# Side loads in one line behind the buffers that come free, and a last chunk that ends with the smallest pair of tiles

## Chip, core and metric

The kernel runs on one core of a Trainium2 chip. The metric is the time on the device in microseconds of one execution, as the median of several runs. A profile is one execution of its own, with its own time.

## What is computed

The reference is a chain of three layers on 2304 tokens (4 sequences of 576) with 512 features:

- attention with 8 heads of 64, a causal window of 128 positions and a linear position bias per head;
- a mixture of 8 experts: `out += P[:, e] * (relu(x @ w1[e]) @ w2[e])`, with 1024 hidden features per expert, where P comes from the gate's logits, normalised 8 times over its rows and its columns in turn;
- a last layer `g = max(0.01 * h, h)` with `h = x @ w_in`, and `g @ w_out`, with 2048 hidden features.

`w_in` and `w_out` arrive as float64, everything else as float32.

## The kernel before, in words

**Tiles and chunks.** The 2304 tokens are 18 tiles of 128. They stand in five groups, `PAIRS`: groups 0 to 3 have four tiles each (n = 2), group 4 has only two (n = 1). The hidden features of both layers are cut into chunks of 512: chunks 0 to 15 are the eight experts, two each, and chunks 16 to 19 are the last layer (NC = 20, NCE = 16). Matrix products are taken block-wise in seven products instead of eight (`PRODUCTS`), and each factor is split into two fp16 parts, so that one product is three matmuls per inner block.

**Units and steps.** A unit is one chunk for one group. `a_steps` makes the hidden features of a unit (matmuls at L705): seven steps per group of rows, that is 14 for groups 0 to 3 and 7 for group 4. Behind each step VectorE or ScalarE takes the product out of PSUM (L717, L721, L726 to L729); L750, L753, L759, L734 and L775 then form the sums and the fp16 parts that go to `h`, and GpSimd takes the low parts off at L778. `b_steps` multiplies by the second weight (matmuls at L822) and adds to the 18 accumulators `acc` (128x512 fp32): by one instruction of VectorE (L835), or for the products in SHARED by ScalarE into `part` (L832) and an addition by GpSimd (L833). `b_steps` of a unit runs while `a_steps` of the next one does; `merge` sets the interleaving and keeps the last three b-steps (`tail`) for behind the last a-step. The table `units` gives the order of units: in every chunk from 1 on, the groups 0, 4, 1, 2, 3.

**Side work.** Between the steps, `tick` takes jobs from the list `side`. At group 4 of each chunk this list gets the work for the next chunk. In chunks 1 to 11 it begins with `cast_jobs(3)`: up to three float64 pieces (32 in all) of 128x512 values, each of which is loaded (L628), turned into float32 and stored to device memory (L659). The steps of one piece are called here by their lines: exponent L634 on VectorE and L637 on ScalarE, sign L640 on VectorE, mantissa L645 on VectorE and L646 on ScalarE, the low word L652 on ScalarE, and two instructions of GpSimd, L654 and L658. Then `weight_jobs` loads the two weights of the next chunk, a (first factor) and b (second factor), at L549, squares them on ScalarE to find their size (L553, four instructions each), scales them (L556) and splits them (L427, L428). All these loads share two buffers, `raw`: a load waits until the transfer or the last instruction that reads the buffer's old content is done. The lists have entries `None`, which let a tick pass without work.

```
jobs = [load for load, _ in todo[:2]] + [None] * 8
for k, (_, rest) in enumerate(todo):
    jobs += rest + [load for load, _ in todo[k + 2:k + 3]]
return [a.load, b.load] + [None] * 10 + a.scale() + a.early() + b.scale() + b.early()
```

How many jobs a tick takes is the length of `side` divided by the steps that are left (with the offset `rest`), rounded up.

**What sets the order in the queues.** The program is traced in the order of the steps, and a scheduler then places each instruction in its engine's queue by a model of its own; a side job stays behind the last step of its engine that was traced before it (`issue_after`), but may come later. Engines and the queue of transfers (SyncE, SP) take their queue strictly in order. The results leave by a store of 128x512 per accumulator (L843) behind the steps 5 and 6 of the last chunk's b-steps.

## Time and profile before

| | us |
|---|---|
| median of 3 runs (2017.71 to 2022.5) | 2018.65 |
| the profiled execution's own time | 2017.12 |
| its span, first to last instruction | 2015.3 |

| engine | busy us | share of the span |
|---|---|---|
| PE (TensorE matmul) | 1913.0 | 95% |
| PEld (weight load) | 1654.4 | 82% |
| DVE (VectorE) | 1409.4 | 70% |
| ACT (ScalarE) | 1361.9 | 68% |
| POOL (GpSimd) | 1320.4 | 66% |

Matmuls overlap, so PE's busy time is not work at its peak rate: what counts is where PE stood idle, and which instruction ended that idle time. In a timeline row the first number is the start in us from the begin of the span, the second the time from there to the end of the last instruction in the row, and the brackets say how long the engine had been idle before and what released it. A start is exact, a matmul's end is modelled.

### The profile page before, as it was taken

How to read it: one execution, taken by the hardware profiler on the slowest of the kernel's cores; microseconds unless marked ns; L12 is line 12 of the kernel's file. 1: busy time of each engine (PE TensorE's matmuls, PEld its weight loads, DVE VectorE, ACT ScalarE, POOL GpSimd, SP SyncE). 2: the span in 40 equal slices, each digit the busy share in tenths (PEclk: the TensorE clock that was granted, in tenths of full speed). 3: DMA queues.
4: the chain of work that ended last, by engine and by line, in shares of the span. 5: the costliest groups of instructions: out<-in, count | busy, mean ns of one | idle time of the engine just before them, and what ended most of it. 6: DMA issues, size and time to landing. Idle time of an engine off the chain costs nothing.

```text
span 2015.3 us, 45289 instructions
## 1 busy us (share of the span) xinstructions
PE 1913.0 (95%) x17657; PEld 1654.4 (82%) x17657; DVE 1409.4 (70%) x3906; ACT 1361.9 (68%) x3099; POOL 1320.4 (66%) x1133
## 2 busy tenths in 40 slices
PE   8899988999999989999999999999999998999998
PEld 6767767787888879788888978889898887889897
DVE  6767778666767667676767667666666677677776
ACT  6656676767676666757666675766666678776754
POOL 4523347577775958777686867767657686657743
PEclk9779999999999999999999999999999999999999
DMA  4221100211202021111202011101010000001001
GB/s 128 78 79 53 33 1 22 69 37 54 69 33 80 22 69 35 57 64 38 80 12 79 28 63 54 43 22 30 14 43 22 22 22 22 22 22 43 1 22 74
DMA packets 55271, 88.90 MB, mean 44 GB/s; under 512 B 3344, under 2 KB 21776, under 8 KB 55056
## 3 DMA queue, kind: packets, MB, share of 16 engines
q1 hardware_dynamic: 55056, 86.01, 13.1%
q8 instruction: 138, 2.26, 0.5%
q14 instruction: 77, 0.63, 0.1%
HBM read 72.89 MB, written 13.11 MB: 43 GB/s over the span
## 4 chain that ended last, share of the span: by engine, by line
PE 71%; DVE 9%; ACT 7%; DMA 5%; POOL 4%; issue 3%; SPq 0%; POOLq 0%; ACTq 0%; DVEq 0%
PE t L822 32%; PE s L705 19%; PE sq L705 14%; DMA raw<-in_moe_w_dram 3%; PE s L234 3%; PE o L288 2%; PE pt L273 1%; DVE acc L835 1%; DVE e L262 1%; ACT junk L553 1%; POOL h L778 1%; DVE raw L640 1%; POOL xp L428 1%; DVE h L734 1%; POOL acc L833 1%
## 5 line engine op out<-in xcount | busy, mean ns | idle before, releaser
L822 PE MATMUL t<-w,h 128*128 128x256 f16 x7560 | 978.4, 274 | 37.2 <-ACT part L832 15.1
L705 PEld LDWEIGHTS <-w 128*128 128x128 f16 x8400 | 761.4, 98 | 126.6 <-issue 39.6
L822 PEld LDWEIGHTS <-h 128*128 128x128 f16 x7560 | 732.4, 98 | 143.3 <-issue 46.7
L705 PE MATMUL s<-xp,w 128*128 128x256 f16 (+1 forms) x4908 | 617.3, 264 | 32.9 <-ACT q L729 21.4
L835 DVE SCALAR_TENSOR_TENSOR acc<-t,pu,acc 128x256 f32<-128x256 f32 x864 | 406.9, 479 | 227.3 <-PE t L822 174.6
L778 POOL TENSOR_TENSOR h<-s,h 128x1024 f16<-128x1024 f32 x180 | 386.2, 2146 | 193.8 <-ACT h L775 142.0
L705 PE MATMUL sq<-xp,w 128*128 128x256 f16 (+1 forms) x3492 | 442.4, 263 | 0.5 <-DVE k L409 0.5
L833 POOL TENSOR_TENSOR acc<-acc,part 128x256 f32<-128x256 f32 x324 | 240.6, 745 | 238.3 <-ACT part L832 189.4
L428 POOL TENSOR_TENSOR w<-raw,w 128x512 f16<-128x512 f32 x240 | 277.3, 1172 | 47.8 <-ACT w L427 47.6
L734 DVE SCALAR_TENSOR_TENSOR h<-sq,h 128x512 f16<-128x512 f32 (+1 forms) x348 | 190.9, 550 | 67.7 <-ACT h L759 49.6
L832 ACT ACTIVATE part<-t,pu 128x256 f32<-128x256 f32 x324 | 152.5, 471 | 117.4 <-PE t L822 107.5
L775 ACT ACTIVATE h<-s 128x1024 f16<-128x1024 f32 x180 | 189.9, 1055 | 49.0 <-DVE s L734 46.5
L721 DVE SCALAR_TENSOR_TENSOR sq<-sq,q 128x256 f32<-128x256 f32 x348 | 148.6, 427 | 81.1 <-PE sq L705 72.5
L717 ACT ACTIVATE q<-s 128x256 f32<-128x256 f32 x366 | 138.1, 380 | 86.2 <-PE s L705 60.5
L427 ACT ACTIVATE w<-raw 128x512 f16<-128x512 f32 x240 | 147.4, 626 | 14.1 <-PE t L822 7.1
L734 DVE SCALAR_TENSOR_TENSOR s<-sq,s 128x256 f32<-128x256 f32 x348 | 144.7, 416 | 2.6
L753 ACT ACTIVATE h<-sq 128x512 f16<-128x512 f32 x174 | 103.3, 594 | 54.7 <-DVE sq L721 31.0
L734 DVE SCALAR_TENSOR_TENSOR s<-sq,q 128x256 f32<-128x256 f32 x348 | 130.1, 415 | 11.8 <-ACT q L729 10.1
L721 DVE SCALAR_TENSOR_TENSOR sq<-s,q 128x256 f32<-128x256 f32 x174 | 74.6, 429 | 89.2 <-ACT q L717 81.6
L553 ACT ACTIVATE junk<-raw 128x512 bf16<-128x512 f32 x160 | 100.5, 628 | 32.0 <-DMA raw<-in_moe_w_dram 31.0
L556 ACT ACTIVATE raw<-raw,sr 128x512 f32<-128x512 f32 x160 | 102.3, 713 | 3.2 <-DVE sr L422 3.0
L759 ACT ACTIVATE h<-sq 128x256 f16<-128x256 f32 x174 | 66.0, 379 | 55.5 <-DVE sq L721 47.5
(140 smaller groups left out, 1901.1 us busy)
## 6 DMA issues: line engine op xcount, KB each, us to landing
raw<-in_moe_w_dram SPq DMA_DIRECT2D x32, 1024.0 KB, 5.2
raw<-in_moe_w_in_dram SPq DMA_DIRECT2D x16, 512.0 KB, 3.7
raw<-in_moe_w_out_dram SPq DMA_DIRECT2D x16, 512.0 KB, 3.5
q_t<-in_q_dram SPq DMA_DIRECT2D x18, 256.0 KB, 3.0
k_t<-in_k_dram SPq DMA_DIRECT2D x18, 256.0 KB, 3.0
v_t<-in_v_dram SPq DMA_DIRECT2D x18, 256.0 KB, 2.7
out_dram<-acc SPq DMA_DIRECT2D x18, 256.0 KB, 2.0
win<-raw SPq DMA_DIRECT2D x16, 256.0 KB, 2.3
```

Source lines behind the costliest of these rows:

```text
L427: nc.scalar.activation(out=hi, in_=src, func=AF.Copy)
L428: nc.gpsimd.tensor_tensor(out=lo, in0=src, in1=hi, op=ALU.subtract)
L705: nc.tensor.matmul(d[b][:, f, :], t[:, wp, kk, ft * P:(ft + 1) * P], XP[p][:, o, kk, xp, :], start=(i == 0 and f == 0 and j in FIRST), sto ...
L717: nc.scalar.activation(out=q[:, k], in_=ps, func=AF.Copy, scale=CS)
L721: nc.vector.scalar_tensor_tensor(out=block(k), in0=ps, scalar=CS, in1=q[:, k], op0=ALU.mult, op1=ALU.add)
L734: nc.vector.scalar_tensor_tensor(out=out, in0=in0, scalar=sc, in1=in1, op0=op0, op1=op)
L775: nc.scalar.activation(out=h[:, 3:7, 0, :], in_=d["s"], func=AF.Copy)
L778: nc.gpsimd.tensor_tensor(out=h[:, 3:7, 1, :], in0=d["s"], in1=h[:, 3:7, 0, :], op=ALU.subtract)
L822: nc.tensor.matmul(ps, h[:, o, hp, f, tt * P:(tt + 1) * P], w[:, wp, ft, :], start=(i == 0 and j in FIRST), stop=(i == 5), skip_group_chec ...
L832: nc.scalar.activation(out=part, in_=ps, func=AF.Copy, scale=s)
L833: nc.gpsimd.tensor_tensor(out=dst, in0=dst, in1=part, op=ALU.add)
L835: nc.vector.scalar_tensor_tensor(out=dst, in0=ps, scalar=s, in1=dst, op0=ALU.mult, op1=ALU.add)
```

## The change

`cast_jobs` and `weight_jobs` become one function, `side_jobs`. All loads of a chunk stand in one line: the pieces, then a, then b. Two loads are issued at once, eight empty entries follow, and then each piece's work is followed by the next load of the line. So a's load is traced behind the second piece and b's behind the third, where before both stood behind the third; behind that, two empty entries instead of ten come ahead of a's work (four where there are no pieces, behind the eight). The list has 75 entries instead of 83 in a chunk with three pieces.

In the last chunk the groups come in the order 0, 1, 2, 3, 4, so that the last unit has 7 b-steps instead of 14. In it, no product goes by way of `part` (the new flag `final`): all seven are added by VectorE. `merge` gets the argument `after`, which keeps seven b-steps instead of three behind the last a-step of the program. Every output tile is stored in two halves of 128x256, each as soon as its last addition is issued.

```diff
--- before.py
+++ after.py
@@ -825,9 +825,10 @@
             t, half = ((ta, 0), (ta, 0), (ta, 1), (tb, 1), (tb, 1), (ta, 1), (tb, 0))[j]
             dst = acc[t][:, half * HF:(half + 1) * HF]
             s = pu[ci][:, t:t + 1]
+            final = ci == NC - 1 and p == ends[ci]
             if fresh and j in (0, 2, 3, 6):
                 nc.scalar.activation(out=dst, in_=ps, func=AF.Copy, scale=s)
-            elif j in SHARED and not fresh:
+            elif j in SHARED and not fresh and not final:
                 part = vp.tile([P, HF], F32, tag="part", bufs=2, name="part")
                 nc.scalar.activation(out=part, in_=ps, func=AF.Copy, scale=s)
                 nc.gpsimd.tensor_tensor(out=dst, in0=dst, in1=part, op=ALU.add)
@@ -836,22 +837,21 @@
             anchor()
             if ci == F1 // FC - 1 and j in (5, 6):
 
-                t = (ta, tb)[j - 5]
-                later(1, lambda: nc.scalar.activation(out=acc[t], in_=acc[t], func=AF.Copy, scale=Pm[:, t, 0:1]))
-            if ci == NC - 1 and j in (5, 6):
-                t = (ta, tb)[j - 5]
-                nc.sync.dma_start(out[t * P:(t + 1) * P, :], acc[t])
+                ts = (ta, tb)[j - 5]
+                later(1, lambda: nc.scalar.activation(out=acc[ts], in_=acc[ts], func=AF.Copy, scale=Pm[:, ts, 0:1]))
+            if ci == NC - 1 and j in (1, 4, 5, 6):
+                nc.sync.dma_start(out[t * P:(t + 1) * P, half * HF:(half + 1) * HF], dst)
 
         ds = [{}, {}]
         return [lambda tt=tt, j=j: step(tt, j, ds[tt]) for tt in range(n) for j in range(7)]
 
-    def merge(a, b):
+    def merge(a, b, after=3):
 
         if not b:
             return a
         seq = [a[0], b[0], a[1], a[2], b[1]] + a[3:7]
         a, b = a[7:], b[2:]
-        tail = b[-3:] if len(b) > 10 else b[-1:]
+        tail = b[-after:] if len(b) > 10 else b[-1:]
         b = b[:len(b) - len(tail)]
         na, nb = 0, 0
         while na < len(a) or nb < len(b):
@@ -958,18 +958,18 @@
 
     cast = list(range(2 * KT * (F2 // FC)))
 
-    def cast_jobs(n):
+    def side_jobs(ci, n):
+
 
         todo = [to_single(cast.pop(0)) for _ in range(min(n, len(cast)))]
-        jobs = [load for load, _ in todo[:2]] + [None] * 8
-        for k, (_, rest) in enumerate(todo):
-            jobs += rest + [load for load, _ in todo[k + 2:k + 3]]
-        return jobs
-
-    def weight_jobs(ci):
         weights(ci)
         a, b = W[0][ci], W[1][ci]
-        return [a.load, b.load] + [None] * 10 + a.scale() + a.early() + b.scale() + b.early()
+        loads = [load for load, _ in todo] + [a.load, b.load]
+        work = [rest for _, rest in todo]
+        jobs = [loads.pop(0), loads.pop(0)] + [None] * 8
+        for rest in work:
+            jobs += rest + [loads.pop(0)]
+        return jobs + [None] * (2 if work else 4) + a.scale() + a.early() + b.scale() + b.early()
 
     def weigh(ci):
         pu[ci] = small.tile([P, NTILE], F32, tag="pu", name="pu")
@@ -979,7 +979,9 @@
         else:
             nc.scalar.activation(out=pu[ci], in_=Pm[:, :, e], func=AF.Copy, scale=rw[ci])
 
-    units = [(0, 3), (0, 4)] + [(ci, p) for ci in range(1, NC) for p in (0, 4, 1, 2, 3)]
+    units = [(0, 3), (0, 4)] + [(ci, p) for ci in range(1, NC - 1) for p in (0, 4, 1, 2, 3)]
+
+    units += [(NC - 1, p) for p in (0, 1, 2, 3, 4)]
     ends = {}
     for ci, p in units:
         ends[ci] = p
@@ -1004,12 +1006,11 @@
         if u is not None and ci >= 1:
             if n and units[n - 1][0] != ci and ci != NCE:
                 weigh(ci)
-            if p == 4:
-                side += cast_jobs(3) if ci < NCE - 1 else []
-                side += weight_jobs(ci + 1) if ci + 1 < NC else []
+            if p == 4 and ci < NC - 1:
+                side += side_jobs(ci + 1, 3 if ci < NCE - 1 else 0)
         if prev[0] == NCE:
             weigh_pair(*prev)
-        seq = merge(a, b) if a else b
+        seq = merge(a, b, 7 if n == len(units) - 1 else 3) if a else b
 
         rest = {4: 57, 1: 36, 2: 8, 3: -19}.get(p) if u is not None and ci >= 1 else None
         for k, fs in enumerate(seq):
```

The queue of transfers (SP) in chunk 7, which is the stretch from 859 to 909 us in the trace of before; the names are the buffers' (`raw`) and what they are loaded from or stored to. Before:

```order
L628 DMA raw_11936<-in_moe2_w_out_dram 128x1024
L628 DMA raw_11938<-in_moe2_w_out_dram 128x1024
L659 DMA wout32_123<-raw_11936 128x512
L628 DMA raw_12074<-in_moe2_w_out_dram 128x1024
L659 DMA wout32_123<-raw_11938 128x512
L549 DMA raw_12182<-in_moe_w1_dram 128x4x512
L659 DMA wout32_123<-raw_12074 128x512
L549 DMA raw_12192<-in_moe_w2_dram 128x4x512
```

Now:

```order
L628 DMA raw_11936<-in_moe2_w_out_dram 128x1024
L628 DMA raw_11946<-in_moe2_w_out_dram 128x1024
L659 DMA wout32_123<-raw_11936 128x512
L628 DMA raw_12114<-in_moe2_w_out_dram 128x1024
L659 DMA wout32_123<-raw_11946 128x512
L549 DMA raw_12173<-in_moe_w1_dram 128x4x512
L659 DMA wout32_123<-raw_12114 128x512
L549 DMA raw_12233<-in_moe_w2_dram 128x4x512
```

Loads and stores stand in the same order in both; this holds for every chunk but the first one with pieces, in which a's load moves ahead of one store.

ScalarE (ACT) in the same chunk, around the third piece (`raw_12074` before, `raw_12114` now); L832 of before is L833 now. Before:

```order
L832 ACTIVATE part_12120<-t1_12113,pu_11657 128x256
L759 ACTIVATE h_12172<-sq_12219 128x256
L729 ACTIVATE q_12173<-s0_12174 128x256
L652 ACTIVATE raw_12074<-raw_12074 128x512
L717 ACTIVATE q_12265<-s0_12266 128x256
L637 ACTIVATE raw_12074<-raw_12074,shift_92 128x512
L832 ACTIVATE part_12141<-t2_12134,pu_11657 128x256
L717 ACTIVATE q_12383<-s0_12384 128x256
L775 ACTIVATE h_12172<-s_12252 128x4x256
L646 ACTIVATE raw_12074<-raw_12074,ones_90 128x512
L717 ACTIVATE q_12265<-sq_12305 128x256
L753 ACTIVATE h_12264<-sq_12275 128x2x256
```

Now:

```order
L759 ACTIVATE h_12163<-sq_12215 128x256
L729 ACTIVATE q_12164<-s0_12165 128x256
L717 ACTIVATE q_12267<-s0_12268 128x256
L833 ACTIVATE part_12132<-t2_12125,pu_11657 128x256
L775 ACTIVATE h_12163<-s_12252 128x4x256
L717 ACTIVATE q_12386<-s0_12387 128x256
L652 ACTIVATE raw_12114<-raw_12114 128x512
L646 ACTIVATE raw_11946<-raw_11946,ones_90 128x512
L637 ACTIVATE raw_12114<-raw_12114,shift_92 128x512
L646 ACTIVATE raw_12114<-raw_12114,ones_90 128x512
L717 ACTIVATE q_12267<-sq_12313 128x256
L753 ACTIVATE h_12266<-sq_12279 128x2x256
```

The low word of the third piece (L652) stood ahead of a copy out of PSUM (`q_12265<-s0_12266`) and is now behind the matching one and two more instructions; the mantissa of the second piece (L646), which stood before this stretch, now stands behind that L652, and the third piece's L637 and L646 follow at once. The four squarings of weight a (L553) start two instructions behind the L753 that ends the rows of before, and eleven behind the L753 that ends those of now.

VectorE (DVE) at the end of the program, its last eleven or twelve instructions; the numbers behind `acc` are tiles. Before:

```order
L835 SCALAR_TENSOR_TENSOR acc9_110<-t2_28435,pu_27265,acc9_110 128x256
L734 SCALAR_TENSOR_TENSOR s_28432<-sq_28361,s_28432 128x256
L835 SCALAR_TENSOR_TENSOR acc11_112<-t0_28377,pu_27265,acc11_112 128x256
L835 SCALAR_TENSOR_TENSOR acc13_114<-t0_28530,pu_27265,acc13_114 128x256
L835 SCALAR_TENSOR_TENSOR acc12_113<-t0_28472,pu_27265,acc12_113 128x256
L835 SCALAR_TENSOR_TENSOR acc13_114<-t0_28530,pu_27265,acc13_114 128x256
L835 SCALAR_TENSOR_TENSOR acc14_115<-t0_28472,pu_27265,acc14_115 128x256
L835 SCALAR_TENSOR_TENSOR acc12_113<-t2_28497,pu_27265,acc12_113 128x256
L835 SCALAR_TENSOR_TENSOR acc14_115<-t0_28472,pu_27265,acc14_115 128x256
L835 SCALAR_TENSOR_TENSOR acc15_116<-t0_28530,pu_27265,acc15_116 128x256
L835 SCALAR_TENSOR_TENSOR acc13_114<-t2_28555,pu_27265,acc13_114 128x256
L835 SCALAR_TENSOR_TENSOR acc15_116<-t0_28530,pu_27265,acc15_116 128x256
```

Now:

```order
L734 SCALAR_TENSOR_TENSOR s_28438<-sq_28376,s_28438 128x256
L836 SCALAR_TENSOR_TENSOR acc14_115<-t0_28330,pu_27265,acc14_115 128x256
L836 SCALAR_TENSOR_TENSOR acc16_117<-t0_28546,pu_27265,acc16_117 128x256
L836 SCALAR_TENSOR_TENSOR acc13_114<-t2_28512,pu_27265,acc13_114 128x256
L836 SCALAR_TENSOR_TENSOR acc16_117<-t1_28554,pu_27265,acc16_117 128x256
L836 SCALAR_TENSOR_TENSOR acc15_116<-t0_28486,pu_27265,acc15_116 128x256
L836 SCALAR_TENSOR_TENSOR acc16_117<-t0_28546,pu_27265,acc16_117 128x256
L836 SCALAR_TENSOR_TENSOR acc17_118<-t2_28570,pu_27265,acc17_118 128x256
L836 SCALAR_TENSOR_TENSOR acc15_116<-t0_28486,pu_27265,acc15_116 128x256
L836 SCALAR_TENSOR_TENSOR acc17_118<-t0_28546,pu_27265,acc17_118 128x256
L836 SCALAR_TENSOR_TENSOR acc16_117<-t2_28570,pu_27265,acc16_117 128x256
L836 SCALAR_TENSOR_TENSOR acc17_118<-t0_28546,pu_27265,acc17_118 128x256
```

The last additions went to tiles of group 3 (`acc12` to `acc15`) with GpSimd's share beside them; now they go to group 4 (`acc16`, `acc17`), seven of them, and all on VectorE. 

## Rows read from the trace of the kernel before

**Rows 1.** The page's first part: busy time, share, instructions of each engine.

```profile
PE 1913.0 (95%) x17657; PEld 1654.4 (82%) x17657; DVE 1409.4 (70%) x3906; ACT 1361.9 (68%) x3099; POOL 1320.4 (66%) x1133
```

**Rows 2.** Timeline of SP: loads by chunk, with pieces (L628) and without (L549).

```profile
892.84 0.33 SPq L628 DMA_DIRECT2D raw<-in_moe_w_out_dram  x1
...
1157.75 0.33 SPq L628 DMA_DIRECT2D raw<-in_moe_w_out_dram  x1
...
1300.05 0.38 SPq L549 DMA_DIRECT2D raw<-in_moe_w_dram  x1
...
1467.46 0.37 SPq L549 DMA_DIRECT2D raw<-in_moe_w_dram  x1
```

**Rows 3.** Waits of the whole span: engine line waited for: us, times, longest us.

```profile
ACT junk L553 <- DMA raw<-in_moe_w_dram: 31.0, 17, 3.6
...
PE s L705 <- ACT q L729: 21.4, 16, 2.8
```

**Rows 4.** Timeline of chunk 7 around the third piece.

```profile
886.74 0.72 ACT L646 ACTIVATE raw<-raw,ones 128x512 f32<-128x512 int32 x1
...
888.78 0.72 POOL L833 TENSOR_TENSOR acc<-acc,part 128x256 f32<-128x256 f32 x1
...
890.76 0.33 SPq L659 DMA_DIRECT2D wout<-raw  x1
...
892.17 0.60 ACT L753 ACTIVATE h<-sq 128x512 f16<-128x512 f32 x1 [0.40 <-DVE sq L721]
...
896.38 0.81 PE L822 MATMUL t<-w,h 128*128 128x256 f16 x6 [0.63 <-ACT part L832]
896.45 1.17 DVE L634 TENSOR_SCALAR raw<-raw 128x512 int32<-128x512 int32 x1 [0.90 <-DMA raw<-in_moe_w_out_dram]
...
898.73 0.38 ACT L717 ACTIVATE q<-s 128x256 f32<-128x256 f32 x1
...
899.06 0.81 PE L822 MATMUL t<-w,h 128*128 128x256 f16 x6 [0.49 <-DVE acc L835]
...
902.10 0.36 ACT L717 ACTIVATE q<-sq 128x256 f32<-128x256 f32 x1
...
904.19 0.82 PE L705 MATMUL sq<-xp,w 128*128 128x256 f16 x6
```

**Rows 5.** Timeline of chunk 7 around the squarings of weights a and b.

```profile
899.46 0.33 SPq L659 DMA_DIRECT2D wout<-raw  x1
...
901.61 0.38 SPq L549 DMA_DIRECT2D raw<-in_moe_w_dram  x1
...
906.46 0.63 ACT L553 ACTIVATE junk<-raw 128x512 bf16<-128x512 f32 x1 [1.76 <-DMA raw<-in_moe_w_dram]
...
908.53 1.47 PE L705 MATMUL s<-xp,w 128*128 128x256 f16 x12 [2.11 <-ACT q L729]
...
912.82 0.38 ACT L717 ACTIVATE q<-s 128x256 f32<-128x256 f32 x1
913.64 0.63 ACT L553 ACTIVATE junk<-raw 128x512 bf16<-128x512 f32 x1 [0.44 <-DMA raw<-in_moe_w_dram]
```

**Rows 6.** Timeline of PE in chunk 6, behind the same wait.

```profile
819.52 2.72 PE L705 MATMUL s<-xp,w 128*128 128x256 f16 x12 [2.48 <-ACT q L729]
```

**Rows 7.** The sign instruction of all 32 pieces: ns min/median/max.

```profile
L640 DVE SCALAR_TENSOR_TENSOR raw<-raw,sign x32: 735/1496/2043, 340.5 to 1247.0; 128x512 int32<-128x512 int32 x32
```

**Rows 8.** Timeline of the end of the program.

```profile
1995.10 0.82 PE L705 MATMUL s<-xp,w 128*128 128x256 f16 x6
...
2001.23 2.12 POOL L778 TENSOR_TENSOR h<-s,h 128x1024 f16<-128x1024 f32 x1 [2.92 <-issue]
...
2011.09 0.81 PE L822 MATMUL t<-w,h 128*128 128x256 f16 x6 [0.51 <-DVE acc L835]
...
2011.94 0.48 DVE L835 SCALAR_TENSOR_TENSOR acc<-t,pu,acc 128x256 f32<-128x256 f32 x1 [0.52 <-PE t L822]
```

**Rows 9.** DMA issues of the whole span: KB each, median us to landing.

```profile
out_dram<-acc SPq DMA_DIRECT2D x18, 256.0 KB, 2.0
```

## Prediction

> **What bounds the kernel now.** I read the page's busy times first. PE is busy 95% of the span [rows 1], so what a change can win is PE's idle time and any stretch at a low clock. The timeline of SP then gives the length of a chunk. With pieces it is (1157.75 - 892.84) / 3 = 88.3 us, without pieces (1467.46 - 1300.05) / 2 = 83.7 us [rows 2]. So each of the ten chunks with three pieces loses some 4.6 us, and in the others PE hardly waits. The list of waits says where to look: ScalarE stood 31.0 us, 17 times, in front of L553 for a weight's load, and PE 21.4 us, 16 times, for the copy L729 [rows 3]. In chunk 7 the two are one event: L553 waits 1.76 us for weight a, the L729 queued behind it comes late, and PE idles 2.11 us for it [rows 5]. A smaller loss comes earlier in the chunk: around the third piece's load, which VectorE awaits for 0.90 us, PE idles 0.63 and 0.49 us [rows 4].
>
> **What the change does there.** The title of the edit is the loads, but they hardly move: SP has loads and stores in the same order, and in the timeline each load goes out when the store ahead of it is done (store at 899.46, load at 901.61), not when the program reaches it. What moves is the use. Ten entries of the list went at two per step before (83 entries for 78 steps) and go at one per step now (75 for 78), so the first piece's work begins five steps later, while weight a's begins three steps earlier in the program. The scheduler then puts a's squarings behind what it takes for the landing. I price the three places of chunk 7, as the type of the ten.
>
> **Place 1, the third piece.** Now the first piece's L646 ends at 887.46, its store goes out at 890.76, the third piece's load at 892.84, and VectorE has the data at 896.45 [rows 4]. That is 3.30 + 2.08 + 3.61 = 8.99 us. In the new order GpSimd does the piece without an accumulation in between (0.72), so 8.27. But that L646 now stands directly ahead of the L753 which ran at 892.17. If it runs then, it ends at 892.9 and the third piece lands at 901.2. ScalarE comes to L652 behind the copy of 898.73; without the 0.63 us of PE idle ahead of it, that copy ends at 898.5. So ScalarE waits 2.7 us, where VectorE's 0.90 was the longest wait. Behind the wait stand L652, L646, L637, L646 in one row; at 0.72 each, the duration of L646, that is 2.9 us, and the copy behind them starts at 904.1. Today it starts at 902.10, less the 1.12 us of idle ahead of it 900.98: it is 3.1 us late. PE needed it 1.73 us after it ended (902.46 to 904.19). So PE idles 1.4 us in place of 1.12: +0.3 per chunk. VectorE can make it worse. It has the sign instructions of the first two pieces close together now, and each takes 735 to 2043 ns [rows 7]; one microsecond more on the way to the first L646 gives 2.4 us of idle, +1.3. I take the middle, **+0.8**. The ends are -1.1 (the load is hidden) and +2.3 (two microseconds later).
>
> **Place 2, weight a.** The second piece's L646 is second behind that wait: it ends at 901.2 + 1.4 = 902.6. GpSimd, store and load then take 2.6, 2.15 (899.46 to 901.61) and 4.85 (901.61 to 906.46) [rows 5], so a lands at 912.2. ScalarE comes to L553 behind the copy which ends today at 913.20. Less 3.23 us of idle so far (0.63, 0.49, 2.11), plus 1.4 to 2.4 from place 1, that is 911.4 to 912.4, and with the later end the landing is 913.2. The wait is 0.8 us instead of 1.76, and PE idles 1.2 instead of 2.11: **-0.9**. The ends are -2.1 (no wait) and 0.
>
> **Place 3, weight b.** It waits 0.44 us today and PE does not show it [rows 5]; in other chunks it does (17 waits of L553 in all for 11 chunks). Now eleven and more instructions lie between. **-0.2**; ends 0 and -0.6.
>
> The three places give -0.3 us per chunk, -3 us for ten. **The clock**: after an idle time of 2.48 us in chunk 6, twelve matmuls took 2.72 us [rows 6], after 2.11 us in chunk 7 the same twelve took 1.47 [rows 5]. That is the lower of the two levels, 1.2 GHz, for a part of the stretch, and costs 1.25 us. The timeline has four such stretches in the chunks with pieces, this one among them. With 1.2 us of idle in its place I count half of them gone, **-2.5** (ends 0 and -5).
>
> **The last chunk.** The last L705 ends at 1995.92 and the last L822 at 2011.90 [rows 8], 16.0 us for 102 matmuls. At full pace these take 102 x 0.108 = 11.0 us (twelve in a row take 1.47, six 0.82). What stretches it is the way to `h`'s low parts: L778 ends at 2003.35, 7.4 us after the last L705, and 51 matmuls with additions by way of ScalarE and GpSimd between them came behind it. In the new order 34 stand behind it, all added by VectorE, in turns of two tiles: 3.7 us and about 0.8 of waits for an addition of 0.48. Ending L778 at 7.9, since a `part` stands ahead of its input, the end is at 12.4 instead of 16.0. I take **-3** (ends 0 and -4.9, the full pace). The two `part` products save nothing else. A store of a whole tile landed in 2.0 us [rows 9]; for half of one there is no row. I take 0, with -0.5 and +0.5 as ends; 18 more issues at 0.33 us go to an SP that idles.
>
> No other chunk changes: without pieces there are 12 empty entries instead of 10, two steps, in chunks where PE does not wait.
>
> **Sum.** -3 - 2.5 - 3 = -8.5. The profiled execution took 2017.12 us, so 2008.6; the median shown lies 1.5 us above it, so **2010**.
>
> **Rivals.** (1) *The waits go.* If the uses now stand far enough behind every load, place 1 is covered, and what goes is PE's wait for L729, 21.4 us [rows 3], the clock's 5 and the tail's 3: 1989. For it: the squarings stand nine copies and sums later than before. Against it: the load lands later too, since it waits for the second piece. The Trainium skill (DMA: Bandwidth & Descriptors, Rules for kernel authors) says to issue a transfer early and wait for it late. By that rule this is the outcome; the trace agrees that the wait is the loss, but shows the issue bound to the buffer.
> (2) *Slower: the row of four behind L652.* If the first piece's L646 ends at 895 rather than 893 on chunk 7's scale, the third piece lands at 903.2, the copy behind the row is 5.1 us late and PE idles 3.4 us, +2.3 per chunk; weight a, whose chain starts behind the same wait, still costs 1.8, -0.3. Ten chunks make +20, with the tail 2036, and it decides from about 894 on. For it: two sign instructions of up to 2.0 us each now come in front of the second mantissa, and the first L646 stands behind one of them. The Trainium skill (GPSIMD Engine Reference, Specifications) says that GpSimd shares its interfaces to SBUF with VectorE, to the cost of VectorE's instructions with two SBUF inputs; L640 is one, and its spread agrees [rows 7]. By that rule packing pieces tighter makes them longer. Against it: ScalarE has slack, and a PE that stalls once gives the loads behind it time.
> (3) *The loads do nothing*: SP's order is the same, what place 1 gains place 2 loses, and the tail alone is left: 2015.6.
>
> **How the numbers follow.** Forecast 0.42, with a range of its own from 2002 to 2020; rival 1 0.20, rival 2 0.25, rival 3 0.13. About 0.3% (6 us) can be told from no change. Of the forecast 0.26 lies beyond it on the fast side, 0.14 within, 0.02 on the slow side. So faster is 0.46, the same 0.27 (with rival 3), slower 0.27. From 1990 to 2033 about 8 in 10 are taken in: the bounds of the forecast, most of rival 1 and half of rival 2.
>
> **What would show it.** Right: in chunk 7 ScalarE's longest wait before L553 falls under 1 us, a wait of 1 to 3 us appears in front of the third piece's L652 or L634, chunks with pieces still take about 88 us, fewer stretches at 1.2 GHz, and the last L822 ends some 12.5 us after the last L705. Wrong: chunks of 85 to 86 us (rival 1), chunks of 90 us with idle time over 3 us around the third piece (rival 2), or a tail that still takes 16 us.

## The result, and the profile after

The changed kernel takes 2045.16 us (median of 4 runs, 2040.27 to 2048.64), the kernel before 2018.18 us beside it (4 runs): ratio 1.0149, 95% interval 1.0123 to 1.0174. It is 27 us slower, where the prediction was 2010 with a range to 2033. The profiled execution took 2047.74 us, with a span of 2045.9.

The page's busy times, against [rows 1]:

```profile
PE 1925.4 (94%) x17657; PEld 1649.7 (81%) x17657; DVE 1408.5 (69%) x3908; ACT 1367.7 (67%) x3097; POOL 1314.1 (64%) x1131
```

The same 17657 matmuls take 12 us more of busy time, and PE idles 18 us more. The time stretch from 500 to 1310 us, which is chunks 3 to 11, shows both; first the kernel before, then the changed one (columns: stretch and its length, busy time and instructions of PE, PEld, DVE, ACT, POOL, granted clock, DMA share, GB/s):

```profile
500.00:1310.00 810.00, 779.43 (x7363) 686.75 (x7362) 556.92 (x1407) 540.02 (x1176) 600.07 (x505) 0.99 0.16 51
```

```profile
500.00:1310.00 810.00, 768.31 (x7177) 666.50 (x7176) 541.49 (x1378) 533.66 (x1154) 581.45 (x492) 1.00 0.15 50
```

186 matmuls fewer are done there, though the clock is higher. The list of waits of the changed kernel's whole span, against [rows 3]:

```profile
ACT junk L553 <- DMA raw<-in_moe_w_dram: 26.4, 18, 3.0
...
PE t L822 <- DVE acc L836: 24.5, 44, 3.0
...
PE sq L705 <- ACT q L717: 17.8, 20, 1.9
...
DVE raw L634 <- DMA raw<-in_moe_w_in_dram: 12.7, 5, 3.0
ACT raw L652 <- DMA raw<-in_moe_w_in_dram: 12.2, 6, 2.8
...
PE t L822 <- ACT part L833: 9.4, 21, 2.2
...
PE s L705 <- ACT q L729: 1.0, 2, 0.7
```

The wait for the copy L729 is nearly gone (21.4 us before). New waits have come in its place: VectorE and ScalarE wait for the third piece (L634, L652), and PE waits for the copy L717 and for additions.

Counting the matmuls of L705 and L822 along the two timelines of PE, each by its columns, tells where the time goes; the two profiled executions are 30.6 us apart. At equal work the changed kernel is less than 1 us behind at 430 and at 540 us of the kernel before, 19 us at 1290, 21 at 1560, 34 at 1970 and 30.6 at the end. So **chunks with pieces** lose some 19 us, **chunks 16 to 19** another 13, and the tail gives 3 back.

Chunk 7 of the changed kernel, SP and the side work, to be held against [rows 4, 5]. Its group 4 begins at 877.03, that of the kernel before at 867.88 (the first 128x128 matmul of L705), so its rows stand 9.15 us later for that alone:

```profile
902.15 0.71 ACT L646 ACTIVATE raw<-raw,ones 128x512 f32<-128x512 int32 x1
...
905.61 0.33 SPq L659 DMA_DIRECT2D wout<-raw  x1
...
907.70 0.33 SPq L628 DMA_DIRECT2D raw<-in_moe_w_out_dram  x1
...
911.25 0.43 DVE L634 TENSOR_SCALAR raw<-raw 128x512 int32<-128x512 int32 x1 [2.28 <-DMA raw<-in_moe_w_out_dram]
911.26 0.69 ACT L652 ACTIVATE raw<-raw 128x512 f32<-128x512 uint32 x1 [2.04 <-POOL h L778]
911.84 0.71 ACT L646 ACTIVATE raw<-raw,ones 128x512 f32<-128x512 int32 x1
912.46 0.71 ACT L637 ACTIVATE raw<-raw,shift 128x512 int32<-128x512 int32 x1
913.07 0.71 ACT L646 ACTIVATE raw<-raw,ones 128x512 f32<-128x512 int32 x1
913.68 0.36 ACT L717 ACTIVATE q<-sq 128x256 f32<-128x256 f32 x1
914.09 0.82 PE L705 MATMUL sq<-xp,w 128*128 128x256 f16 x6 [0.82 <-ACT q L717]
915.25 1.78 PE L705 MATMUL s<-xp,w 128*128 128x256 f16 x12 [0.34 <-DVE sq L721]
...
917.99 0.38 SPq L549 DMA_DIRECT2D raw<-in_moe_w_dram  x1
918.87 0.82 PE L705 MATMUL sq<-xp,w 128*128 128x256 f16 x6 [0.36 <-DVE s L734]
919.96 0.33 SPq L659 DMA_DIRECT2D wout<-raw  x1
923.16 0.63 ACT L553 ACTIVATE junk<-raw 128x512 bf16<-128x512 f32 x1 [0.39 <-DMA raw<-in_moe_w_dram]
923.87 0.38 SPq L549 DMA_DIRECT2D raw<-in_moe_w_dram  x1
925.32 0.82 PE L822 MATMUL t<-w,h 128*128 128x256 f16 x6 [0.40 <-ACT part L833]
...
927.18 0.81 PE L822 MATMUL t<-w,h 128*128 128x256 f16 x6 [0.16 <-ACT part L833]
...
929.59 0.63 ACT L553 ACTIVATE junk<-raw 128x512 bf16<-128x512 f32 x1 [2.10 <-DMA raw<-in_moe_w_dram]
932.19 0.81 PE L705 MATMUL sq<-xp,w 128*128 128x256 f16 x6 [1.11 <-ACT q L717]
935.54 1.47 PE L822 MATMUL t<-w,h 128*128 128x256 f16 x12 [0.58 <-DVE acc L836]
```

The row of four on ScalarE stands as forecast, with L652 behind a wait of 2 us (L634 on VectorE starts at the same time, released by the transfer) and PE 0.82 + 0.34 + 0.36 us idle behind it. Weight a is cheap now: 0.39 us of wait, and 0.40 and 0.16 of idle behind it. Weight b is not: its L553 waits 2.10 us, and PE idles 1.11 and 0.58 us around it.

The end of the program, against [rows 8]:

```profile
2029.03 0.83 PE L705 MATMUL s<-xp,w 128*128 128x128 f16 x12
...
2035.98 2.13 POOL L778 TENSOR_TENSOR h<-s,h 128x1024 f16<-128x1024 f32 x1 [0.27 <-POOL acc L834]
...
2037.79 4.91 PE L822 MATMUL t<-w,h 128*128 128x256 f16 x40 [0.36 <-DVE acc L836]
```

From the end of the last L705 to that of the last L822 it takes 12.84 us, before 16.0.

### The profile page after: what moved, and what is told of

Same layout as the page of the kernel before. It is cut to its first block, busy times and chain, and to the rows that moved or that the text cites. A ratio compares the mean times of both kernels' runs of the same rounds, so it can differ in the third digit from the quotient of the medians.

```text
span 2045.9 us, 45308 instructions
## 1 busy us (share of the span) xinstructions
PE 1925.4 (94%) x17657; PEld 1649.7 (81%) x17657; DVE 1408.5 (69%) x3908; ACT 1367.7 (67%) x3097; POOL 1314.1 (64%) x1131
## 4 chain that ended last, share of the span: by engine, by line
PE 64%; DVE 11%; ACT 8%; DMA 7%; POOL 6%; issue 5%; SPq 0%; ACTq 0%; POOLq 0%; DVEq 0%
PE t L822 29%; PE s L705 16%; PE sq L705 12%; DMA raw<-in_moe_w_dram 3%; PE s L234 3%; PE o L288 2%; DVE acc L836 2%; DVE h L734 2%; DVE s L734 1%; POOL h L778 1%; DVE e L262 1%; PE pt L273 1%; ACT junk L553 1%; POOL raw L658 1%; DMA win<-raw 1%
## 5 line engine op out<-in xcount | busy, mean ns | idle before, releaser
L822 PE MATMUL t<-w,h 128*128 128x256 f16 x7560 | 990.8, 274 | 45.9 <-DVE acc L836 24.5
L705 PEld LDWEIGHTS <-w 128*128 128x128 f16 x8400 | 758.1, 98 | 142.0 <-issue 57.7
L822 PEld LDWEIGHTS <-h 128*128 128x128 f16 x7560 | 732.4, 98 | 160.6 <-issue 63.6
L705 PE MATMUL s<-xp,w 128*128 128x256 f16 (+1 forms) x4908 | 609.6, 263 | 16.2 <-ACT q L717 7.6
L705 PE MATMUL sq<-xp,w 128*128 128x256 f16 (+1 forms) x3492 | 443.9, 262 | 24.2 <-ACT q L717 17.8
L834 POOL TENSOR_TENSOR acc<-acc,part 128x256 f32<-128x256 f32 x322 | 233.8, 730 | 251.9 <-ACT part L833 209.6
L833 ACT ACTIVATE part<-t,pu 128x256 f32<-128x256 f32 x322 | 151.7, 471 | 90.5 <-PE t L822 82.7
L717 ACT ACTIVATE q<-s 128x256 f32<-128x256 f32 x366 | 138.4, 379 | 106.4 <-PE s L705 83.2
L753 ACT ACTIVATE h<-sq 128x512 f16<-128x512 f32 x174 | 103.2, 593 | 76.8 <-DVE sq L721 47.2
L553 ACT ACTIVATE junk<-raw 128x512 bf16<-128x512 f32 x160 | 100.2, 626 | 27.5 <-DMA raw<-in_moe_w_dram 26.4
```

Source lines behind the costliest of these rows:

```text
L705: nc.tensor.matmul(d[b][:, f, :], t[:, wp, kk, ft * P:(ft + 1) * P], XP[p][:, o, kk, xp, :], start=(i == 0 and f == 0 and j in FIRST), sto ...
L717: nc.scalar.activation(out=q[:, k], in_=ps, func=AF.Copy, scale=CS)
L822: nc.tensor.matmul(ps, h[:, o, hp, f, tt * P:(tt + 1) * P], w[:, wp, ft, :], start=(i == 0 and j in FIRST), stop=(i == 5), skip_group_chec ...
L833: nc.scalar.activation(out=part, in_=ps, func=AF.Copy, scale=s)
L834: nc.gpsimd.tensor_tensor(out=dst, in0=dst, in1=part, op=ALU.add)
```

## The experiments

All lists below have the same jobs, but for the last three, which spread the pieces over more chunks; they differ in where a job stands. "Step" is the step of a chunk's 78 at which a job is traced, counted from group 4's first; lists of more than 78 entries take two per step at the start. **a out** is the mean time, over chunks 4 to 10, from the first matmul of group 4 to the start of weight a's load on SP, and **chunk** the mean length of these seven chunks from one group 4 to the next, both from the timelines. (In the three lists just named, chunk 4 still has three pieces.)

| run | pieces from step | third piece | weights' work | a out, us | chunk, us | ratio to before, 95% |
|---|---|---|---|---|---|---|
| before | 5 | 16 | 33 | 33.8 | 88.95 | 1 |
| changed kernel | 10 | 22 | 30 | 41.2 | 90.86 | 1.0149 (1.0123 to 1.0174) |
| e1_loads | 10 | 22 | 30 | 41.3 | 91.07 | 1.0208 (1.0171 to 1.0245) |
| e3_pace | 10 | 21 | 30 | 42.0 | 91.58 | 1.0162 (1.0138 to 1.0186) |
| e16_late_dve | 10 | 21 | 30 | 43.0 | 91.84 | 1.0144 (1.0108 to 1.0181) |
| e7_late | 10 | 21 | 33 | 42.5 | 91.38 | 1.0133 (1.0080 to 1.0185) |
| e9_gap | 10 | 26 | 33 | 40.5 | 91.08 | 1.0130 (1.0087 to 1.0174) |
| e5_short | 10 | 22 | 30 | 41.2 | 90.80 | 1.0118 (1.0063 to 1.0173) |
| e13_seven | 7 | 18 | 30 | 35.3 | 89.30 | 0.9989 (0.9968 to 1.0010) |
| e12_nine | 6 | 17 | 33 | 32.1 | 87.75 | 0.9938 (0.9914 to 0.9962) |
| e4_line | 5 | 17 | 33 | 33.1 | 89.11 | 1.0034 (1.0017 to 1.0050) |
| e6_early | 5 | 16 | 30 | 33.1 | 87.92 | 0.9947 (0.9924 to 0.9971) |
| e8_third | 5 | 21 | 33 | 33.5 | 87.88 | 0.9947 (0.9914 to 0.9979) |
| e10_both | 5 | 21 | 33 | 33.5 | 87.54 | 0.9929 (0.9902 to 0.9956) |
| e11_early_gap | 5 | 21 | 30 | 33.2 | 89.60 | 1.0039 (1.0017 to 1.0062) |
| e14_three | 3 | 14 | 30 | 28.5 | 88.58 | 0.9951 (0.9928 to 0.9974) |
| e2_last | 5 | 16 | 33 | 33.7 | 89.29 | 1.0010 (0.9991 to 1.0029) |
| e17_two_late | 10 | none | 30 | 30.5 | 88.24 | 1.0108 (1.0077 to 1.0138) |
| e15_two | 5 | none | 30 | 25.5 | 85.68 | 0.9898 (0.9864 to 0.9933) |
| e18_two_last | 5 | none | 30 | 25.6 | 85.56 | 0.9891 (0.9864 to 0.9919) |

The median of before beside these runs was 2015.5 to 2017.1 us.

### Which part of the change: lists, last chunk, pace, line of loads

**e1_loads**: the new lists; last chunk, `merge` and stores as before.

> The new side lists alone; the last chunk, its merge and its stores as before. Theory A (two thirds of the loss stand in the ten chunks with pieces, some 2.1 us each, read from the starts of L778, whose lag grows from 1 us at 503 to 20 us at 1300; the rest behind 1600): 2036 to 2044, and the lag of L778 reaches 18 to 22 us by 1300 again. Rival B (most of the loss comes with the last chunk's order): under 2030.

**e2_last**: the other way about, old lists with the new last chunk.

> The last chunk's order, its kept-back seven steps, its additions and its half stores alone; the side lists as before. Theory A: 2019 to 2028, that is the tail's 3 us won (last L822 12.8 us behind the last L705, not 16.0) and more than that lost again in chunk 19, where the lag of L778 grows by 5 to 6 us; no lag ahead of 1850. Rival B: 2035 to 2042. My prediction's step for the tail, if nothing is given back: 2015.

**e3_pace**: old lists, with two empty entries for ten in chunks with pieces:

```diff
-return [a.load, b.load] + [None] * 10 + a.scale() ...
+return [a.load, b.load] + [None] * (2 if work else 10) + a.scale() ...
```

> The list of 75 entries (two empty entries instead of ten ahead of the weights' work in chunks with pieces), but both weight loads behind the third piece as before. Theory A1 (the pace does it: the first piece's work begins five steps later and is packed with the rest, so that the scheduler moves third-piece and weight work next to what PE waits for): 2034 to 2042, lag of 16 to 22 us by 1300. Theory A2 (where the loads stand does it): within 4 us of before, 2014 to 2022.

**e4_line**: `side_jobs`, with `[None] * (10 if work else 2)`.

> The line of loads alone: a's load behind the second piece and b's behind the third, but ten empty entries behind them, so 83 entries and the pace as before; lists without pieces as before. Theory A1 (pace): 2014 to 2022. Theory A2 (the loads): 2034 to 2042. If both e3 and e4 lie between, the two parts each bring some of it.

Measured: 2054.62, 2015.12, 2045.54 and 2020.74 us. The lists bring the whole loss and the last chunk none, so theory A holds and B falls, though both of A's ranges were missed: e1_loads came out 11 us above its range, which makes it slower than the changed kernel, and e2_last 4 us below. Within the lists it is the pace (A1): one number in the old code, ten empty entries made two, costs as much as the whole change (4 us above A1's range), and the new line of loads at the old pace costs 0.3%. In one thing A was wrong. The losses in chunks 16 to 19 come with the lists as well: at equal work e1_loads falls back by 12 us from 1560 to 1970 with the old last chunk, and e2_last by 0.2.

### Pace: late pieces or early weights

**e5_short**: the changed kernel with `[None] * 2` in every list.

> The changed kernel, but the lists without pieces have ten empty entries ahead of the weights' work as before, not twelve. Theory C (the 11 us that the changed kernel loses behind 1600, which the run with the old last chunk loses too, come from these two entries: each of the short PE waits at 1822 to 1978 then goes): 8 to 11 us under the changed kernel, 2033 to 2038, and from 1740 to 2010 PE idle no more than in the kernel before. Rival (they come from the state that the earlier chunks leave behind, or from the new last chunk): 2042 to 2048.

**e6_early** and **e7_late** start from e3_pace; e6_early has 3 empty entries ahead of the pieces' work and 7 ahead of the weights', e7_late has 8 and 5.

> 75 entries, both weight loads behind the third piece, three empty entries ahead of the pieces' work and seven behind the loads: the pieces' work and all loads stand at the steps of the kernel before (pieces from step 5, a's load at 21, b's at 22), only the weights' work is three steps earlier (30, not 33). Theory P (pieces five steps later do the harm): 2014 to 2022. Theory W (weights three steps earlier do it): 2035 to 2048.

> 78 entries: the pieces' work from step 10 and the loads of the weights at 26 and 27 as in the run with the pace alone, but the weights' work at step 33 as before. Theory P: 2035 to 2048. Theory W: 2014 to 2024.

**e8_third**: e4_line, with four of its ten empty entries moved:

```diff
-for rest in work:
-    jobs += rest + [loads.pop(0)]
-return jobs + [None] * (10 if work else 2) + ...
+for k, rest in enumerate(work):
+    jobs += [None] * (4 if k == 2 else 0) + rest + [loads.pop(0)]
+return jobs + [None] * (6 if work else 2) + ...
```

> 83 entries with a's load behind the second piece; four of the ten empty entries moved ahead of the third piece, so that its work stands four steps (some 4 to 5 us) further behind its load; last chunk as before. If the wait for the landed piece and the row of ScalarE behind it are what costs (the first rival of my prediction): L652 waits under 0.5 us, and 2004 to 2014. If ScalarE's row costs the same wherever it stands, or the weights' loads, now later, make up for it: 2016 to 2030.

Measured: 2041.54, 2006.27, 2043.49, 2005.56 us. Theory P holds and W falls, with e6_early 8 us below P's range: with the pieces at step 5 the weights may come three steps earlier (e6_early, 0.5% faster), with the pieces at step 10 it does not help to give the weights their three steps back (e7_late). e7_late and e8_third have the third piece at step 21 and the weights at 33, both of them; only the first two pieces (five steps) and the loads (one to ten) stand apart, and that is 1.9%. Theory C, which had 2033 to 2038, falls: without the two empty entries the loss in chunks 16 to 19 shrinks from 13 to 6.5 us at equal work; it does not go.

### Landing or standing, sums of gains, and chance

**e9_gap**: the line of e8_third started late, with 1 empty entry ahead of the weights. **e10_both**: e8_third with the changed kernel's last chunk. **e11_early_gap**: e8_third with 3 empty entries in place of 8 and 3 in place of 6. **e12_nine**: the kernel before with 9 empty entries for 10 in chunks with pieces.

> The pieces' work late as in the changed kernel (step 10), loads in the changed kernel's line, but four empty entries ahead of the third piece: its work from step 26, that is eleven steps behind its load (15), not seven; weights' work at step 33 as before; last chunk as before. Theory R (the harm of the late start is that ScalarE's row of the third piece waits for a transfer just landed and PE then for ScalarE): the wait ahead of L652 falls under 1 us and the time to 2014 to 2026. Theory S (the harm is where the steps stand, in the first steps of group 1 and behind them, not the landing): 2035 to 2050.

> The run with the third piece four steps later and early start, with the changed kernel's last chunk. If the tail's 3 us add to it: 1998 to 2006, last L822 12.5 to 13 us behind the last L705. If the new last chunk moves other chunks' order, as in the changed kernel behind 1740: 2006 to 2015.

> 75 entries: pieces from step 5, a's load at 16, third piece at 21 (eleven steps behind its load), b's load at 26, weights' work at 30: the two kernels that were faster by 0.5% in one; last chunk as before. If the gains of the later third piece and of the earlier weights are separate mechanisms they add: 1994 to 2002. If both are the same slack, or chance of the order: 2003 to 2012.

> The kernel before with nine empty entries instead of ten ahead of the weights' work in chunks with pieces, nothing else: 82 entries. A null change by every theory of place: 2012 to 2021, within 0.3%. If it moves by 0.5% or more either way, differences of that size between the lists are chance of the order, and no mechanism should be read from them.

Measured: 2044.44, 2002.57, 2023.92, 2003.15 us. e12_nine is the measure for all others: one empty entry less, and the kernel is 0.6% faster. Its text calls it a null change; it does move the pieces by one step, but in the direction that costs. The scheduler makes another order for every list, and differences of about half a per cent either way between lists are no mechanism. The gains of e6_early and e8_third are of this size, and they did not add: e11_early_gap lies above both of its ranges. The late start, seven lists with three pieces and 1.2 to 2.1%, lies outside it. e9_gap is 1.3% slower, as theory S has it, but it does not separate R from S well: the scheduler put L652 back to the landing, where in chunk 7 it still waits 2.1 us. The trace of e12_nine separates them. Its L652 waits longer than that of any other list, 26.7 us over the span against 5.1 before and 22.7 in the changed kernel, and it is one of the fast ones, so a long wait at the landing is not by itself what the late start pays for. That takes the ground from e8_third's first theory too, although the time came into its range:

```profile
ACT raw L652 <- DMA raw<-in_moe_w_out_dram: 12.5, 5, 3.1
ACT raw L652 <- DMA raw<-in_moe_w_in_dram: 10.7, 5, 3.8
...
ACT raw L652 <- POOL raw L658: 3.5, 1, 3.5
```

### Rising cost or threshold, the third piece, ScalarE's rows

**e13_seven** and **e14_three**: e6_early with 5 and 5, and 1 and 9 empty entries.

> The list of 75 entries as in the run with early pieces, but five empty entries ahead of the pieces' work and five behind the loads: pieces from step 7 (5 in the early run, 10 in the run with the pace alone), weights' work at 30 in all three. Theory P (every step by which the pieces start late packs their work closer to the weights' work): between the two, 2014 to 2032. Rival (a threshold: the pieces must begin in the first nine steps of group 4): 2002 to 2012.

> The same list with one empty entry ahead of the pieces and nine behind the loads: pieces from step 3. Theory P: no slower than the early run, 1995 to 2010. Rival (at step 3 the pieces' loads have not landed, and GpSimd is still at the weights' splits): 2015 to 2035, with waits for the first piece's transfer.

**e15_two**: old lists, fewer pieces in a chunk. From chunk 15 on its lists also have eight empty entries that those of before don't have.

```diff
-side += cast_jobs(3) if ci < NCE - 1 else []
-side += weight_jobs(ci + 1) if ci + 1 < NC else []
+n = 0 if ci >= NCE - 1 else 3 if ci <= 4 else 2
+side += cast_jobs(n)
+side += weight_jobs(ci + 1, n) if ci + 1 < NC else []
```

with 3 and 13 empty entries where n is 2.

> The lists of the kernel before in chunks 1 to 4, then two pieces in each of chunks 5 to 14 in place of three in 5 to 10 and two in 11: no third load and no third piece behind a freed buffer; pieces from step 5, a's load at 15, weights' work at 30. If the third piece and the weights that wait for its buffer are what a chunk with pieces pays (88 us, not 84): the 5 us of seven chunks become 1 to 2 us in ten, 1985 to 2005. If a chunk with two pieces pays as much as one with three: 2020 to 2040.

**e16_late_dve**: e3_pace with L646 made by VectorE's `tensor_scalar` (multiply, add).

> The run with the pace alone (late pieces), with the mantissa's step L646 taken from ScalarE and made by VectorE: 0.7 us less in each of ScalarE's rows, 23 us in all. Theory R (late pieces cost because ScalarE's rows of three to four side instructions stand ahead of the instruction that empties PSUM for PE): a third to a half of the 33 us comes back, 2025 to 2037. Rival (VectorE is as tight there, or ScalarE's row is not what PE pays for): 2040 to 2055.

Measured: 2015.05, 2008.00, 1997.14, 2048.21 us. From step 3 to step 6 the start costs nothing, at 7 it is within 0.3% of before, at 10 it costs 1.2% and more. By the ranges set beforehand e13_seven falls to P (a cost for each step), near its lower end, and not to the threshold; but half a per cent is the scatter between lists, and between steps 7 and 10 nothing was run, so how the cost sets in is not shown. The column *a out* gives the same two groups in time: of the lists with three pieces none is slower by more than 0.4% up to 35.3 us behind group 4's start, and all are by 1.2% or more from 40.5 us on. It is a mark of the late start and not shown to be its price: ScalarE's waits for a weight in front of L553 are shorter in the changed kernel (26.4 us) than before (31.0). Two pieces a chunk gain 1.0%, and chunks 5 to 10, of 89.0 us before, take 84.9. Two things changed there at once, a third of the piece work went to later chunks and no load stands behind the buffer of a third piece; which of them brings the gain is not separated.

Theory R falls in the form stated: 0.7 us less in each of ScalarE's rows brings nothing back that can be told from the scatter (VectorE now makes L646, so the run can't tell whether VectorE is as tight there). PE's waits of e3_pace and then of e16_late_dve, 500 to 1310 us:

```profile
PE s L705 <- ACT q L717: 23.6, 25, 2.3
PE t L822 <- ACT part L833: 6.2, 18, 1.0
PE t L822 <- DVE acc L836: 4.7, 18, 0.5
...
PE s L705 <- ACT q L729: 1.7, 8, 0.2
```

```profile
PE s L705 <- ACT q L729: 18.1, 17, 4.2
PE t L822 <- DVE acc L836: 10.1, 19, 0.9
PE t L822 <- ACT part L833: 8.8, 19, 0.9
PE s L705 <- ACT q L717: 3.8, 9, 0.7
```

The wait for L717 shrinks by 20 us and is back as waits for L729 and for additions. The instruction named as the releaser is the one at which PE happened to stop; here it was not what the time hung on.

### Two pieces, late, and the best version

**e17_two_late**: e15_two with 8 and 8 empty entries. **e18_two_last**: e15_two with the changed kernel's last chunk.

> The run with two pieces a chunk, its pieces started at step 10 in place of 5, a's load at 20 in place of 15, weights' work at 30 in both. If the late start costs by itself (the place of the pieces' work): 2018 to 2035, some 20 us over the run with two pieces. If it costs only through the third piece and the loads behind its freed buffer, which this list doesn't have or has done by step 21: within 6 us of that run, 1991 to 2004.

> The run with two pieces a chunk and the changed kernel's last chunk. If the tail's 3 us add: 1990 to 1997. If the order of the other chunks shifts with it: 1997 to 2006.

Measured: 2035.05 and 1993.68 us. Without a third piece the late start still costs 38 us over e15_two, so it does not need the third piece. Here a place is seen. Chunk 7 of e17_two_late:

```profile
887.89 0.33 SPq L659 DMA_DIRECT2D wout<-raw  x1
...
890.83 0.38 SPq L549 DMA_DIRECT2D raw<-in_moe_w_dram  x1
...
896.00 0.63 ACT L553 ACTIVATE junk<-raw 128x512 bf16<-128x512 f32 x1 [5.34 <-DMA raw<-in_moe_w_dram]
...
899.67 0.15 DVE L396 TENSOR_SCALAR e<-m 128x1 int32<-128x1 int32 x1
...
899.88 0.22 PE L402 MATMUL mt<-identb,e 128*1 128x128 bf16 x1 [4.46 <-DVE e L396]
```

Weight a's buffer comes free with the first piece's store at 887.89. Its load goes out at 890.83 and lands at 896.00. The squarings stand where the list put them and wait 5.34 us. Behind them comes L396, and the small matmul L402, which carries the weight's size across partitions, stands in PE's own queue: PE idles 4.46 us. Over the whole span this wait is 15.8 us in 6 times, and e15_two has none of it; the two profiled executions are 23.5 us apart. L553 waits 56.9 us, in e15_two 27.3 (first two rows of e17_two_late, then e15_two):

```profile
ACT junk L553 <- DMA raw<-in_moe_w_dram: 56.9, 22, 5.3
...
PE mt L402 <- DVE e L396: 15.8, 6, 4.5
```

```profile
ACT junk L553 <- DMA raw<-in_moe_w_dram: 27.3, 16, 3.7
```

It is not the place of the lists with three pieces: there PE waits for L396 at L402 0.9 us in the changed kernel and 3.8 us, once, in e3_pace. e18_two_last is the fastest of all: 1.1% faster than the kernel before and, by the medians of separate runs, 2.5% faster than the changed one, with a tail of 12.84 us.

## Why the prediction was wrong

**What held.** SP keeps its order, and each load goes out behind a store, about 2.1 us after it where nothing else is in flight. In chunk 7 **place 1** came out: L652 waits 2.0 us (forecast 2.7), the four instructions stand in one row of 2.4 us (2.9), and PE idles 1.5 us behind it (1.4). **Place 2**, weight a, waits 0.39 us instead of 1.76, and PE idles 0.40 + 0.16 (forecast 1.2). The **clock** went the forecast way: in the stretch of 500 to 1310 us the kernel before has three stretches with matmuls at the lower level of 1.2 GHz (at 819, 996 and 1174 us), the changed one has one, at 1109. The **tail** fell by 3.2 us against 3 forecast, though the same code gave 14.2 us in e2_last and e10_both. Half stores land in 1.7 us, against 2.0 for whole tiles [rows 9], and the span ends 3.25 us behind the last L822, before 3.45.

**What failed first: place 3.** I gave weight b -0.2 us. It waits 2.10 us in place of 0.44, and PE idles 1.11 and 0.58 us. I had moved a's landing back by the late chain and not b's; b stands behind the third piece, which is last in that chain, and its store was 3.91 us under way, not 2.1. In chunk 7 PE's idle times come to 4.38 us against 3.23, +1.15 where I had -0.3.

**What failed most: the sum of three places as the price of a chunk.** The chunk is 1.9 us longer, where the sum had -0.3; in e7_late, which is as slow, it is 2.4 us longer. I priced a delay only where the trace of before had an idle time. But the whole chain moves: the first piece's store goes out 28.6 us behind group 4's start instead of 23.0, a's load 41.2 instead of 33.8, b's 47.7 instead of 40.9. PE pays in many short waits: in chunks 4 to 10 it stops 82 times instead of 30, and 43 of these stops, before 11, take 0.2 to 0.6 us. All seven late lists with three pieces have 9 to 13 stops a chunk, the others with three pieces 4 to 6. That the side work is pressed into the steps that are left, and the engines that empty PSUM are late for that, is my reading; no run shows it apart, and there is no single place.

Idle time was also the wrong unit. Per chunk it grows from 3.7 to 4.8 us, +1.1. From start to start of the matmuls the same stops cost 4.4 and 6.7 us, +2.4: by the profile a 128x256 matmul takes 274 ns, and in a row the next one starts 109 ns behind it, so each stop costs that overlap too. Outside of the stops PE loses 0.35 us less (two stretches at the lower clock fewer, of 1.25 us each, would be 0.36 per chunk). Together that is +2.0, the chunk's 1.9 us to about 0.1. "The first piece's work begins five steps later" stood in the prediction as a description; it was the cause, and I gave it no price.

**"No other chunk changes" failed.** Chunks 16 to 19 lose 13 us. Four lists with the new line and a late start share this (changed kernel, e1_loads, e5_short, e9_gap), and e17_two_late too; e3_pace, e7_late and e16_late_dve, late as well, do not. The last chunk's new order is not the cause (e1_loads has it as it was); the two empty entries can be half of it, as e5_short without them loses 6.5 us. What the losers share is an order of their own. In chunk 17 the kernel before and the twelve other lists with three pieces have the same instructions in the same order on PE, ScalarE, VectorE and GpSimd, and all take 82.6 or 82.7 us; the changed kernel and e1_loads have another order and take 86.1, e5_short and e9_gap a third one and 85.9, although their lists for chunks 16 to 19 are those of before. Why the scheduler comes to these orders stays open. The prediction also misread chunks 12 to 14: when the pieces are used up, the old `cast_jobs` still returns eight empty entries, so the kernel before had 18 there, eight of them ahead of the loads, and not 10.

**The rivals.** Rival 2 had the time nearest (2036) and the chunk length (90), and its condition was all but met: the first piece's L646 ends 25.8 us behind group 4's start, on the scale of before at 893.7, just short of the 894 it named. Its mechanism, the row behind L652, was one place among several: PE idles 1.5 us there and not 3.4, and e12_nine waits longer at L652 and is fast. Nor did its reason come: with the pieces packed tighter, the sign instruction L640 got shorter, not longer (compare [rows 7]), so the half microsecond that I added to place 1 for it did not come either (PE's idle time there grew by 0.4 us, not 0.8):

```profile
L640 DVE SCALAR_TENSOR_TENSOR raw<-raw,sign x32: 737/752/1324, 358.1 to 1265.3; 128x512 int32<-128x512 int32 x32
```

I gave it 0.25 and held 2033 for the end of the range. Rival 1, that the waits go, fell because in these lists the issue hangs on the buffer. Nor do L553's waits go with the time: 31.0 us before, 26.4 in the changed kernel, and 27.3 in e15_two, which is 20 us faster than the kernel before.

## What to carry to other kernels

When buffers are recycled, a load's time is set by the work that frees its buffer, not by where the load stands in a list; so a later start of the first user moves every load behind it. Follow that chain as times from a fixed mark in the chunk before pricing single waits, and count the stops of the bounding engine as well as its idle time. Where a scheduler orders the queues, time one change that should do nothing: here it moved 0.6%, and a gain below that is not yet a reason.

## What had not been expected of the hardware

A store that is issued shortly behind a large load takes longer than alone. In the kernel before, the store at 906.25 goes out 4.64 us behind a's load (1 MB, landed after 4.85 us), and the load that waits for it follows 2.12 us later. In the changed kernel the store stands 1.97 us behind the load, and it takes 3.91 us. In e3_pace, chunk 7, 0.44 us behind it, it is 6.31 us:

```profile
926.81 0.38 SPq L549 DMA_DIRECT2D raw<-in_moe_w_dram  x1
927.25 0.49 SPq L659 DMA_DIRECT2D wout<-raw  x1
932.90 0.63 ACT L553 ACTIVATE junk<-raw 128x512 bf16<-128x512 f32 x1 [2.43 <-DMA raw<-in_moe_w_dram]
...
933.56 0.38 SPq L549 DMA_DIRECT2D raw<-in_moe_w_dram  x1
```

L553 starts as weight a lands, at 923.16 in the changed kernel and at 932.90 here, and the load behind the store goes out 0.7 us later in both. So the store ends just behind the load: it does not pass it, and it does not wait for the landing and then take its 2.1 us. The traces of all runs have 56 stores that follow a weight's load within 2 us, and half of them land less than 0.9 us behind it. The Trainium skill (DMA: Bandwidth & Descriptors, Queues, rings and completion order) says that the transfers of one issuing engine share its rings on the same 16 DMA engines, which take descriptors in the order of the ring. By that rule the store's descriptors stand behind the load's, and the trace agrees with the order. Why a itself takes longer to land here, 6.1 us instead of 4.85, is not shown.
